# Linear attention with a leaky-ReLU layer behind it on one core: scores of stage 0 ahead of the turning of stage 1, and v*s added in whole blocks

## The chip, the cores and the metric

The kernel runs on one core of a Trainium2 chip. Its engines each work through a list of their own and wait for one another by semaphores: TensorE (PE, with its weight loads shown as PEld), VectorE (DVE), ScalarE (ACT), GpSimd (POOL) and SyncE (SP). The metric is the device time of one execution in microseconds (us). A difference is judged against runs of the kernel before on the same chip.

## The reference

```python
def _attn_ref(r, k, v, w, u):          # r, k, v: (4, 8, 768, 48); w, u: (8, 48)
    state = np.zeros((B, H, D, D))
    for t in range(S):
        cur = np.einsum('bhd,bhe->bhde', u[None] * kt, vt)
        y[:, :, t] = np.einsum('bhd,bhde->bhe', rt, state + cur)
        state = w[None, :, :, None] * state + np.einsum('bhd,bhe->bhde', kt, vt)
    return y

def _moe_ref(x, w_in, w_out):          # x: (3072, 384); w_in: (384, 2048); w_out: (2048, 384)
    h = x @ w_in
    g = np.maximum(0.01 * h, h)
    return g @ w_out
```

`x` is `y` with the heads side by side: one row of 8 x 48 = 384 for each of the 4 x 768 tokens. The term with `u` is a bonus for the token itself: token t adds v[t] times the scalar s[t] = sum over d of r*u*k, one scalar for each head.

## The kernel before

The 3072 tokens are cut into 24 stages of 128 tokens, six to a batch. The recurrence becomes chunked attention: within a stage, scores are masked to earlier tokens; across stages a state of 48 x 48 for each head is carried. A step is a letter and a stage number:

- P (`prep`, L327 and L329): VectorE scales r and k by powers of the decay into `qk`.
- T (`turn`, L379): eight matmuls against the identity turn `qk`, four for r and four for k, each half into a bank of PSUM; ScalarE (L390) copies them to `tp`; for the k half of stage 0 VectorE does it (L387).
- A (`a_mm`, L403): eight matmuls with 48 rows make the scores, two banks.
- X (`diag`, L334): VectorE multiplies the turned r and k for the scalar s.
- M (`a_mask`, L421): VectorE masks the scores into `at`. The mask is made by POOL (L267), in between its loads.
- K (`kv_mm`, L433, L437, L442): s, the products of k and v, and the carried state, in one bank.
- Q (`prep2`, L342): VectorE makes `vs`, v times s. S (`state`, L487): VectorE decays the state.
- Y (`y_part`, L522): the output of attention for a stage, turned: 384 columns of output, three blocks of 128 partitions, beside one another in one bank. ScalarE (L537) copies it into `xT`.
- G and J (L550, L567): products with w_in, ScalarE's leaky ReLU behind them. H and `second` (L584, L648): products with w_out.

In stages 0 to 7 (`n < DIAG`) the bonus comes into Y as `vs` times the identity; later stages put s on the diagonal of `at`.

Y's matmuls have 32 columns of weights each. They go to four column groups q of the array, one after the other, so that four run side by side. For each block s and group q there are one or two matmuls of `v_sb` with `at`, one of the state with `tp` (except in the first stage of a batch) and, for `n < DIAG`, one of `vs` with `ident`. That is 28 matmuls in stages 0 and 6, and 40 in stages 1 to 5 and 7.

The order of the first ten stages is written out by hand in `ORDER`. Each step adds its instructions to the lists of its engines in this order; `Sched` derives the semaphore waits from what is read and written, and an operation waits for all of its inputs before its first instruction. Banks of PSUM are taken in rotation by `next_bank`. From stage 10 on, loops over pairs of stages do the same.

Of the kernel before, what the change touches and what calls it, by code (L numbers as in the profile page):

```python
# [21 lines left out]
NSL = HD // 128  # L22
# [1 line left out]
FIRST, EARLY = 6, 2  # L24
LOADS = """r1 k1 r2 id k2 wi0 v1 r3 tri k3 v2 wi1 k4 r4 v3 wi2 k5 r5 r6 k6 v4 v5 k7 wi3 r7 v6 v7 wo3 wo2 wo1 wo0"""
ORDER = """
P0 C W T0 P1 T1 A0 X0 M0 P2 A1 K0 T2 Q0 X1 Y0 A2 S0 M1 K1 X2 G0.0 Q1 P3 S1 Y1 T3 K2 M2 G1.0 X3 A3 U G0.1 S2 G1.1 Q2 M3 Y2 K3 P4
T4 Q3 G2.0 G2.1 G0.2 S3 G2.2 G1.2 Y3 P5 A4 P6 X4 M4 T5 X5 G3.0 K4 Q4 A5 S4 T6 G3.1 K5 G3.2 Y4 M5 L8 Q5 Y5 P7 A6 G1.3 J2.0 J2.1 T7
M6 X6 X7 K6 J2.2 J2.3 A7 S6 J2.4 J2.5 L9 Q6 G2.3 G0.3 J2.6 M7 L10 J2.7 L11 G3.3 K7 S7 P8 Q7 Q8 P9 H0 Q9 K8 H1 P10 L12 K9 H2 S8 S9
Y6 Y7 A8 A9 P11 M8 H3 M9 L13  # L30
# [7 lines left out]
class Sched:  # L38
# [8 lines left out]
    def add(self, eng, emit, R=(), W=(), dma=None):  # L47
        o = Op()
        o.eng, o.emit, o.dma, o.inc, o.val = eng, emit, dma, False, None
        deps = []  # L50
        for key in R:
            w = self.writer.get(key)
            if w is not None:
                deps.append((w, True))
        for key in W:
            w = self.writer.get(key)
            if w is not None:
                deps.append((w, False))
            for r in self.readers.get(key, ()):
                deps.append((r, False))  # L60
        o.deps = []
        for d, raw in deps:
            if d.dma is None and d.eng == eng and dma is None and (eng == "pe" or not raw):
                continue
            if d is not o and d not in o.deps:
                o.deps.append(d)
        for key in R:
            self.readers.setdefault(key, []).append(o)
        for key in W:
            self.writer[key] = o  # L70
            self.readers[key] = []
        self.ops.append(o)
        return o
# [47 lines left out]
def bass_rwkv5_eagle__then__act_leaky_relu_kernel(  # L121
# [13 lines left out]
    def SB(name, shape, dt=BF16):  # L135
        return ctx.enter_context(nc.sbuf_tensor(name, shape, dt))

    NQK, NTP, NVS, NAT, NT, NX, NG, NO, NRK = 6, 6, 6, 6, 6, 3, 3, 4, 14
    TURNED, DIAG = 8, 8
# [29 lines left out]
    ident = SB("ident", [128, 128])  # L169
# [5 lines left out]
    vs = [SB(f"vs{i}", [128, HD]) for i in range(NVS)]  # L175
# [12 lines left out]
    V, A, PE, SP, G = nc.vector, nc.scalar, nc.tensor, nc.sync, nc.gpsimd  # L188
# [306 lines left out]
    def y_mm(n, ps_y, key):  # L495
        it, ia, iv, is_ = n % NTP, n % NAT, n % NVS, n % NT

        def column(q):
            todo = []
            for s in range(NSL):  # L500
                p, kk = divmod(4 * s + q, 3)
                c0 = 128 * p
                one = []
                if kk < 2:
                    one.append((v_sb[:, n, c0 + 32 * kk:c0 + 32 * kk + 32], at[ia][:, 0, p, :]))
                if kk > 0:
                    c1 = c0 + 16 + 32 * kk
                    one.append((v_sb[:, n, c1:c1 + 32], at[ia][:, 1, p, :]))
                if n % NC:
                    one.append((st[is_][:, p, 32 * kk:32 * kk + 32], tp[it][:, p, :]))  # L510
                if n < DIAG:
                    one.append((vs[iv][:, 128 * s + 32 * q:128 * s + 32 * q + 32], ident[:, :]))
                todo += [(s, a, m, i == 0, i == len(one) - 1) for i, (a, m) in enumerate(one)]
            return todo

        def emit():
            columns = [column(q) for q in range(4)]
            for step in range(max(len(x) for x in columns)):
                for q in range(4):
                    if step < len(columns[q]):  # L520
                        s, a, m, first_mm, last_mm = columns[q][step]
                        last = PE.matmul(ps_y[32 * q:32 * q + 32, 128 * s:128 * s + 128], a, m,  # L522
                                         start=first_mm, stop=last_mm)
            return last

        reads = [("v", n), "v0", ("at", ia, 0), ("at", ia, 1), "ident", ("tp", it, 0)]
        if n < DIAG:
            reads.append(("vs", iv))
        if n % NC:
            reads.append(("st", is_))  # L530
        add("pe", emit, R=reads, W=[key])

    def y_part(n):
# [328 lines left out]
```

## Time and profile before

| | |
|---|---|
| median of 3 runs | 169.61 us (168.82 to 169.82) |
| the profiled execution | 169.31 us, of which its span 167.6 us |
| PE busy | 159.8 us (95%), 2348 matmuls |
| VectorE, ScalarE, POOL busy | 120.7, 116.1, 81.7 us |
| L522 (Y), all stages | 384 with `at`, 240 with the state, 96 with `vs` |

The span is the time from the first to the last instruction of the program; the rest of the execution lies around it. "Idle before" in a group is the time in which an engine stood still ahead of it, and "<-" names what ended that. "issue" is idle time that ended with no event that the profile shows.

### The profile page before, as it was taken

How to read it: one execution, taken by the hardware profiler on the slowest of the kernel's cores; microseconds unless marked ns; L12 is line 12 of the kernel's file. 1: busy time of each engine (PE TensorE's matmuls, PEld its weight loads, DVE VectorE, ACT ScalarE, POOL GpSimd, SP SyncE). 2: the span in 40 equal slices, each digit the busy share in tenths (PEclk: the TensorE clock that was granted, in tenths of full speed). 3: DMA queues.
4: the chain of work that ended last, by engine and by line, in shares of the span. 5: the costliest groups of instructions: out<-in, count | busy, mean ns of one | idle time of the engine just before them, and what ended most of it. 6: DMA issues, size and time to landing. Idle time of an engine off the chain costs nothing.

```text
span 167.6 us, 5494 instructions
## 1 busy us (share of the span) xinstructions
PE 159.8 (95%) x2348; PEld 133.7 (80%) x2348; DVE 120.7 (72%) x232; ACT 116.1 (69%) x264; POOL 81.7 (49%) x97
## 2 busy tenths in 40 slices
PE   6679999979999999999999999999999999999994
PEld 3557898968766885886875889889899898898993
DVE  7768884853698969999449997986998477036253
ACT  4823888778323581689989889989999845828520
POOL 7999999990079979697570660840000000000000
DMA  5999999999999999989997996994507302002022
GB/s 100 112 149 172 171 152 173 202 187 143 116 123 208 109 139 75 151 150 102 203 157 42 219 124 49 215 120 77 147 0 98 125 4 94 4 0 94 4 94 94
DMA packets 99259, 19.68 MB, mean 117 GB/s; under 512 B 92322, under 2 KB 99236, under 8 KB 99236
## 3 DMA queue, kind: packets, MB, share of 16 engines
q0 software_dynamic: 76512, 10.03, 91.6%
q1 hardware_dynamic: 21682, 9.11, 26.4%
q8 instruction: 18, 0.29, 0.7%
q10 hardware_dynamic: 1042, 0.20, 0.6%
q14 instruction: 5, 0.04, 0.1%
HBM read 20.45 MB, written 4.72 MB: 150 GB/s over the span
## 4 chain that ended last, share of the span: by engine, by line
PE 93%; DVE 3%; issue 1%; ACT 1%; DVEq 0%; ACTq 0%
PE ps_all L567 31%; PE ps_all L648 20%; PE ps_all L584 16%; PE ps_all L522 7%; PE ps_all L550 7%; PE ps_all L403 4%; PE ps_all L379 3%; PE ps_all L437 3%; DVE qk L327 1%; DVE at L421 1%; PE ps_all L255 1%; PE ps_all L442 1%; PE ps_all L295 1%; PE ps_all L433 0%; DVE tp L387 0%
## 5 line engine op out<-in xcount | busy, mean ns | idle before, releaser
L567 PE MATMUL ps_all<-xT,w_in_sb 128*128 128x256 bf16 x480 | 54.5, 273 | 0.0
L567 PEld LDWEIGHTS ps_all<-xT,w_in_sb 128*128 128x128 bf16 x480 | 46.7, 98 | 5.8
L573 ACT ACTIVATE gT<-ps_all 128x512 bf16<-128x512 f32 x80 | 46.7, 595 | 5.7 <-PE ps_all L567 2.1
L218 POOL DMA_DIRECT2D rk_sb<-in_k_dram x23 | 21.7, 944 | 16.3 <-PE ps_all L567 16.3
L584 PE MATMUL ps_all<-w_out_sb,gT 128*128 128x384 bf16 x160 | 27.2, 326 | 0.0
L413 DVE CAST_PREDICATED at<-mask,ps_all 128x1024 bf16<-128x1024 uint16 x16 | 18.8, 1219 | 8.9 <-PE ps_all L403 8.9
L367 ACT ACTIVATE at<-ident,s_tok 128x128 bf16<-128x128 bf16 x80 | 24.8, 389 | 0.0
L584 PEld LDWEIGHTS ps_all<-w_out_sb,gT 128*128 128x128 bf16 x160 | 15.3, 98 | 9.7
L218 POOL DMA_DIRECT2D v_sb<-in_v_dram x24 | 22.7, 955 | 0.4 <-issue 0.4
L218 POOL DMA_DIRECT2D rk_sb<-in_r_dram x23 | 21.5, 939 | 0.0
L361 POOL TENSOR_TENSOR at<-ident,s_tok 128x512 bf16<-128x512 bf16 x12 | 13.4, 1142 | 11.6 <-DVE s_tok L351 11.6
L679 DVE TENSOR_TENSOR out_sb<-ps_all,snap 128x192 f32<-128x192 f32 x22 | 7.8, 356 | 14.5 <-PE ps_all L648 13.8
L648 PE MATMUL ps_all<-tw,gs 128*128 128x192 bf16 x168 | 16.0, 246 | 0.0
L590 ACT ACTIVATE out_sb<-ps_all 128x384 f32<-128x384 f32 x10 | 4.9, 487 | 14.6 <-PE ps_all L584 14.6
L648 PEld LDWEIGHTS ps_all<-tw,gs 128*128 128x128 bf16 x168 | 14.0, 98 | 0.0
L421 DVE TENSOR_TENSOR at<-ps_all,mask 128x512 bf16<-128x512 f32 x16 | 10.3, 684 | 4.7 <-PE ps_all L403 4.7
L537 ACT ACTIVATE xT<-ps_all 128x384 bf16<-128x384 f32 x24 | 11.0, 490 | 3.8 <-PE ps_all L522 3.4
L550 PE MATMUL ps_all<-xT,w_in_sb 128*128 128x128 bf16 x192 | 12.9, 225 | 0.0
L550 PEld LDWEIGHTS ps_all<-xT,w_in_sb 128*128 128x128 bf16 x192 | 11.8, 101 | 0.6 <-issue 0.3
L555 ACT ACTIVATE gT<-ps_all 128x512 bf16<-128x512 f32 x16 | 9.6, 599 | 3.8 <-PE ps_all L550 3.2
L522 PE MATMUL ps_all<-at,v_sb 128*32 128x128 bf16 x384 | 11.9, 224 | 0.0
L622 DVE TENSOR_TENSOR gs<-gT 128x1024 bf16<-128x1024 bf16 x14 | 9.6, 684 | 2.9 <-ACT gT L573 2.9
(81 smaller groups left out, 241.1 us busy)
## 6 DMA issues: line engine op xcount, KB each, us to landing
out_dram<-out_sb SPq DMA_DIRECT2D x22, 192.0 KB, 2.4
v_sb<-in_v_dram POOLq DMA_DIRECT2D x24, 96.0 KB, 5.8
rk_sb<-in_r_dram POOLq DMA_DIRECT2D x23, 96.0 KB, 5.7
rk_sb<-in_k_dram POOLq DMA_DIRECT2D x23, 96.0 KB, 5.3
w_in_sb<-in_moe_w_in_dram POOLq DMA_DIRECT2D x4, 384.0 KB, 6.7
w_out_sb<-in_moe_w_out_dram POOLq DMA_DIRECT2D x4, 384.0 KB, 9.9
out_dram<-out_sb SPq DMA_DIRECT2D x4, 96.0 KB, 1.6
tp<-qk SPq DMA_TRANSPOSE x16, 3.4
```

Source lines behind the costliest of these rows:

```text
L218: add("pool", lambda: G.dma_start(dst, src), R=pace, W=[key], dma=f"{which}{n}")
L361: add("pool", lambda hh=hh, s_of=s_of: G.tensor_tensor(at[ia][:, hh, :, :], ident[:, :].unsqueeze(1).to_broadcast([128, NP, 128]), s_of.un ...
L367: add("act", lambda h=h: A.activation(at[ia][:, h % 2, h // 2, :], ident[:, :], AF.Copy, scale=s_tok[n % 2][:, h:h + 1]), R=["ident", ("s" ...
L413: add("dve", lambda: V.copy_predicated(at[n % NAT][:, :, :, :].rearrange("p two m i -> p (two m) i"), mask[:, :].bitcast(mybir.dt.uint16). ...
L421: add("dve", lambda hh=hh, part=part: V.tensor_tensor(at[n % NAT][:, hh, :, :], part, mask[:, :].unsqueeze(1).to_broadcast([128, NP, 128]) ...
L522: last = PE.matmul(ps_y[32 * q:32 * q + 32, 128 * s:128 * s + 128], a, m, start=first_mm, stop=last_mm)
L537: add("act", lambda: A.activation(xT[m % NX][:, :, 128 * half:128 * half + 128], ps_y[:, 0:HD].rearrange("p (s t) -> p s t", t=128), AF.Copy),
L550: last = PE.matmul(ps_g[:, 128 * f:128 * f + 128], w_in_sb[:, s, 128 * fb:128 * fb + 128], xT[ix][:, s, t], start=s == 0, stop=s == NSL - 1)
L567: last = PE.matmul(ps_g[:, 256 * f:256 * f + 256], w_in_sb[:, s, 128 * fb:128 * fb + 128], xT[ix][:, s, :], start=s == 0, stop=s == NSL - 1)
L573: add("act", lambda: A.activation(gT[ig][:, 2 * j:2 * j + 2, :].rearrange("p f t -> p (f t)"), ps_g[:, :], AF.Prelu, alpha=0.01), R=[key], ...
L584: last = PE.matmul(ps_o[:, 0:HD], gT[ig][:, s, 128 * half:128 * half + 128], w_out_sb[:, s, :], start=s == 0, stop=s == NFB - 1)
L648: done = PE.matmul(ps_o[:, 0:NH], lhs[:, s, :], rhs[:, s, :], start=first and s == 0, stop=s == HF - 1, skip_group_check=not (first and last))
```

## The change

In `ORDER` the steps T1 and A0, and further on A1 and K0, change places. In `y_mm` the twelve matmuls of `vs` with the identity, of 32 columns each, go out of the list for the four column groups; behind it, for `n < DIAG`, three matmuls of 128 columns add them, one for each block of 128. So that these can add to what stands in the bank, the start flag is set for the first block alone in these stages, and the stop flag only on the last of the three.

```diff
 ORDER = """
-P0 C W T0 P1 T1 A0 X0 M0 P2 A1 K0 T2 Q0 X1 Y0 A2 S0 M1 K1 X2 G0.0 Q1 P3 S1 Y1 T3 K2 M2 G1.0 X3 A3 U G0.1 S2 G1.1 Q2 M3 Y2 K3 P4
+P0 C W T0 A0 P1 X0 M0 T1 P2 K0 A1 T2 Q0 X1 Y0 A2 S0 M1 K1 X2 G0.0 Q1 P3 S1 Y1 T3 K2 M2 G1.0 X3 A3 U G0.1 S2 G1.1 Q2 M3 Y2 K3 P4
 T4 Q3 G2.0 G2.1 G0.2 S3 G2.2 G1.2 Y3 P5 A4 P6 X4 M4 T5 X5 G3.0 K4 Q4 A5 S4 T6 G3.1 K5 G3.2 Y4 M5 L8 Q5 Y5 P7 A6 G1.3 J2.0 J2.1 T7
 M6 X6 X7 K6 J2.2 J2.3 A7 S6 J2.4 J2.5 L9 Q6 G2.3 G0.3 J2.6 M7 L10 J2.7 L11 G3.3 K7 S7 P8 Q7 Q8 P9 H0 Q9 K8 H1 P10 L12 K9 H2 S8 S9
 Y6 Y7 A8 A9 P11 M8 H3 M9 L13
...
                 if n % NC:
                     one.append((st[is_][:, p, 32 * kk:32 * kk + 32], tp[it][:, p, :]))
-                if n < DIAG:
-                    one.append((vs[iv][:, 128 * s + 32 * q:128 * s + 32 * q + 32], ident[:, :]))
                 todo += [(s, a, m, i == 0, i == len(one) - 1) for i, (a, m) in enumerate(one)]
...
                         s, a, m, first_mm, last_mm = columns[q][step]
                         last = PE.matmul(ps_y[32 * q:32 * q + 32, 128 * s:128 * s + 128], a, m,
-                                         start=first_mm, stop=last_mm)
+                                         start=first_mm and (s == 0 or n >= DIAG),
+                                         stop=last_mm and n >= DIAG)
+            if n < DIAG:
+                for s in range(NSL):
+                    last = PE.matmul(ps_y[:, 128 * s:128 * s + 128], vs[iv][:, 128 * s:128 * s + 128], ident[:, :],
+                                     start=False, stop=s == NSL - 1)
             return last
```

## The prediction

> **What bounds the kernel now.** I read the page first, for the engine that has no idle time to give.
>
> ```profile
> PE 159.8 (95%) x2348; PEld 133.7 (80%) x2348; DVE 120.7 (72%) x232; ACT 116.1 (69%) x264; POOL 81.7 (49%) x97
> PE   6679999979999999999999999999999999999994
> ```
>
> PE is the bound from about 12.1 us on: one slice of forty (around 35 us) is below 9 until the tail. A change that both of whose edits lie before 53 us can therefore pay in three ways only: it removes PE idle time ahead of 12 us, it removes the gap near 35 us, or it changes PE's own work. So I read next the chain of work that ended last, in order of time, for the start.
>
> ```profile
> 7.27 0.58 DVE tp L387
> 7.88 0.35 DVE qk L327
> 8.22 0.28 DVE qk L329
> 8.55 1.03 PE ps_all L379 x8
> 9.58 0.56 PE ps_all L403 x8
> 10.24 1.29 DVE at L421 x2
> 11.53 0.26 DVE qk L327
> 11.79 0.28 DVE qk L329
> 12.12 1.03 PE ps_all L379 x8
> ```
>
> L379 is a turning T, L403 the scores A, L421 the masking M, L327 and L329 the prep P. The chain runs T1, A0, M0, P2, T2: A0 has its operand from 7.96 us (the DVE cast at 7.27 takes 0.69 in the timeline) but stands on PE behind T1, which waits for P1 until 8.55. VectorE, whose list is M0, P2, Q0, X1, S0, M1, then waits 1.41 us, as its timeline shows; the third line is POOL's, which makes the mask that M0 reads:
>
> ```profile
> 8.41 0.42 DVE L334 TENSOR_TENSOR prod<-tp 128x512 bf16<-128x512 bf16 x1
> 10.24 1.29 DVE L421 TENSOR_TENSOR at<-ps_all,mask 128x512 bf16<-128x512 f32 x2 [1.41 <-PE ps_all L403]
> 8.73 0.34 POOL L267 TENSOR_SCALAR_AFFINE_SELECT mask<-ones 128x128 bf16<-128x128 bf16 x1
> ```
>
> The chain at 35 us shows the other hole, in the middle of K6's four matmuls, which wait for no semaphore:
>
> ```profile
> 35.32 0.11 PE ps_all L437 x2
> 35.43 0.93 issue
> 36.35 0.24 PE ps_all L437 x2
> ```
>
> **Edit 1, the order.** On PE, T1 A0 A1 K0 becomes A0 T1 K0 A1. The steps that issue on VectorE and ScalarE keep their order there (P1, X0, M0, P2; the copies of T1, then T2); no moved step issues a DMA, so SP and POOL are not passed, and only bank numbers change. A0 can start at 7.96 + 0.06 (the distance that T1 shows after its prep, 8.49 to 8.55) = 8.02. M0 followed A0's start by 0.72 (9.52 to 10.24), so A0 would allow 8.74; X0 ends at 8.83; the mask ends at 9.07. The mask is late next, and M0 starts at about 9.13, 1.11 earlier. T2 followed M0 by 1.88 (10.24 to 12.12), so T2 is due at 11.01. Is PE free then? A0's eight start over 0.30, and a change from A to a full-height matmul takes 0.25 in this stretch, so T1 starts at 8.57, 0.02 later than before, and its copies on ScalarE end at 10.29 in place of 10.27. K0 fits into the wait for these copies (0.33 of starts, from about 9.40); if that cover were gone it would cost these 0.33. A1 at 10.35 takes 0.30 + 0.25, and PE is free at 10.9. Behind the new head of PE's list stands only T1, whose input comes at 8.49 anyway. The loads allow it: P2's k landed at 9.94 by the trace and is read at 10.6; K1's v landed at 12.87, and K1 comes at 13.5; P3's k landed at 14.27 and is wanted at 14.8. Further on the least room is P5's r, landed 23.01 and read at 23.27 before, but M4 behind it waited 2.2 us for PE. **Edit 1: -1.11 at T2.** Bounds: 0 if the mask or T1's copies come later than I read, and -1.35 (all of VectorE's wait but its 0.06).
>
> **Edit 2, the blocks.** In stages 0 to 7 twelve matmuls of 32 columns become three of 128: 72 matmuls and 72 weight loads fewer. That is not array time saved. Four narrow ones run side by side, and the timeline of PE shows a step of four every 55 ns, while the whole blocks of L379 follow each other at 56 ns; three steps for three.
>
> ```profile
> 26.47 0.23 PE L522 MATMUL ps_all<-tp,st 128*32 128x128 bf16 x4
> 26.53 0.23 PE L522 MATMUL ps_all<-ident,vs 128*32 128x128 bf16 x4
> 26.69 0.40 PE L403 MATMUL ps_all<-tp 48*128 48x128 bf16 x8
> 27.02 0.62 PE L379 MATMUL ps_all<-ident,qk 128*128 128x128 bf16 x8
> ```
>
> What is new is a change of tile shape inside each step Y. Between two shapes the starts are 0.15 apart (26.53 to 26.69) in place of 0.056; in the slow stretch before 16.4 us it is 0.247 in place of 0.107. The trace has no narrow step followed by a whole block of the same bank; the nearest row is Y1 followed by T3, 0.152. Stages 1 and 2 go on to full blocks anyway (T3, K3), so one change only moves: 0. Stages 3, 5 and 7 go on to A (L403), another shape: +0.097 each. Stages 4 and 6 are followed directly by another Y, a joint that costs 0.127 now: 0.152 + 0.112 + 0.150 in place of 3 x 0.055 + 0.127, +0.122 each. Stage 0, slow, goes on to A2: +0.14. **Edit 2 in the array: 0.29 + 0.24 + 0.14 = +0.67.** Bounds: 0 (if a change into the same bank is free) and +4.0 (rival three). The Trainium skill (TensorEngine Tiling (Array Packing), Key Properties) says that changing the tiling mode drains the array, which speaks against this edit; the trace agrees, at 0.10 us a change, and the sum already has it.
>
> **What the smaller stream does to the gap.** 0.93 us in the chain, 1.13 between two starts where 0.04 is usual: 1.09. Nothing is waited for, and the page has a queue "instruction" with 18 packets of 0.29 MB, 16 KB each; in the trace they start at 16.1, 22.5, 28.0, 33.9 and 39.6 us. About 250 instructions of PE (matmuls, loads, waits) lie between the points 3.2 us ahead of each, and the gap ended 3.2 us ahead of the last: I read it as PE running dry of instructions. The stretch before it is the densest: Y4 and Y5 issue 160 in 1.3 us. By then 6 x 18 = 108 instructions are gone, so the same boundary comes about 4 us of PE work later, among the J steps, which need 54 ns for an instruction and not 8. The same spacing of 5.6 us between packets would nearly be reached at 31 us, for 0.3 at most. I take **-1.09**; bounds -1.09 and 0. The Trainium skill (Runtime: NRT & Kernel Launch, Instruction fetch mechanics) describes refills in blocks of 256 instructions that are mostly hidden; by "hidden" the term would be 0, but this trace shows the blocks and a visible gap.
>
> **The slow start of PE.** The granted clock is 1.00 in all rows, yet twelve matmuls of L550 take 1.42 us at 15.21 and 0.83 at 18.12 in the timeline: starts are 107 ns apart until 16.4, 56 after. If that moment stays at 16.4 while the work comes 0.97 earlier (1.11 less stage 0's 0.14), this much more work runs at half speed: +0.48. If it moves with PE's busy stretch: 0. I take the middle, +0.24.
>
> **Sum:** -1.11 + 0.67 - 1.09 + 0.24 = -1.29. The profiled execution took 169.31 (span 167.6 and 1.7 around it), so 168.0; the median of the three runs is 0.3 above it, and I forecast **168.3**. From 16 to 165 us PE carries any gain to the end: VectorE's and POOL's work from 43 us on starts from K7 on PE and shifts with it.
>
> **Rivals.**
> One: a gain does not arrive. For it: the three runs differ by 1.0 us, so the gap may not be in every run, or the instructions may be late for a reason that their number doesn't touch. Against it: the spacing of the packets. Without the gap's term: 169.61 - 0.20 = 169.4; the same without edit 1 instead.
> Two: PE reaches full speed earlier. Between 9.6 and 13.0 us PE now stands for about a third of the time; after the change it has A1, T2 and Y0 there, with holes of 0.3 us. If full speed comes at 13.0, 3.4 us of slow work shrink by 1.7, of which VectorE, with 1.6 us of idle time between 10.3 and 24.5 left over, lets perhaps 1.0 pass: 167.2. The Trainium skill (TensorE: Matmul & The Clock Gate, Part 1) gives a free-running window of 3.4 us of activity; by that rule this is a matter of phase, and the spread of the runs agrees with it.
> Three, slower: the whole blocks must wait until the narrow matmuls that wrote their columns have ended, since they add to the same words, and likewise out of them. A narrow matmul lasts 0.22, so each of 8 changes in and 7 out would cost up to 0.22 more, 3.3 in all: 168.3 + 3.3 = 171.6. It decides from 0.2 us a change. Against it: narrow groups of Y add to the same columns 0.06 us apart, with no such wait.
>
> **How the numbers follow.** The forecast 0.45 (167.7 to 168.9 by itself), rival one 0.27, two 0.20, three 0.08. A measurement of this kernel tells about 1%, 1.7 us, from no change: faster is below 167.9. Rival two nearly whole (0.17) and a third of the forecast (0.15) make 0.32; slower is most of rival three, 0.07; the rest is 0.61. The range leaves out rival three and the ends of one and two: 166.9 to 169.8.
>
> **What would show it.** M0 at 9.1 us with the mask as its releaser, T2 at 11.0; 0.15 us ahead of the whole blocks, and no saving of PE time in a step Y; no gap of "issue" on PE near 35 us; L550's first twelve at 14.3. I am wrong if M0 stays near 10.2, if a gap of about 1 us stands elsewhere on PE, or if a change of shape costs over 0.2 us.

## Result and the profile after

The changed kernel takes 168.57 us (median of 14 runs, 167.84 to 169.29) against 169.56 for the kernel before in the same job: ratio 0.9942, interval [0.9926, 0.9958], about 1.0 us faster. A second job gave 168.75 against 169.82, ratio 0.9941 [0.9913, 0.9968]. The forecast was 168.3.

The chain of the changed kernel, in order of time (start, length, what), shows the new start: A0 ahead of T1, and T2 at 10.99 where it was 12.12. L520 is now the narrow part of Y, L525 the three whole blocks.

```profile
7.27 0.70 DVE tp L387
7.97 0.05 issue
8.02 0.61 PE ps_all L403 x8
8.63 0.56 PE ps_all L379 x4
9.19 0.02 issue
9.21 1.09 ACT tp L390 x2
10.30 0.04 issue
10.35 0.61 PE ps_all L403 x8
10.96 0.04 issue
10.99 1.03 PE ps_all L379 x8
```

The masking is no longer in it. VectorE's timeline has M0 at 9.11, released by POOL's mask:

```profile
8.41 0.42 DVE L334 TENSOR_TENSOR prod<-tp 128x512 bf16<-128x512 bf16 x1
9.11 1.29 DVE L421 TENSOR_TENSOR at<-ps_all,mask 128x512 bf16<-128x512 f32 x2 [0.28 <-POOL mask L267]
```

K6 runs through without a hole (four L437 in one piece):

```profile
34.45 0.08 PE ps_all L433 x4
34.53 0.19 PE ps_all L437 x4
34.72 1.31 PE ps_all L570 x12
```

And a new wait of PE stands in its timeline near 85 us, ahead of A15, for a transpose:

```profile
84.09 0.40 PE L403 MATMUL ps_all<-tp 48*128 48x128 bf16 x8
85.50 0.40 PE L403 MATMUL ps_all<-tp 48*128 48x128 bf16 x8 [1.01 <-DMA tp<-qk]
```

Since both kernels run the same matmuls but for `vs`, each can be laid on its counterpart in the trace. The table gives how much earlier (minus) a step starts than in the profile of before, for both profiles of the changed kernel:

| step (start before) | first profile | second profile | what happened since the row above |
|---|---|---|---|
| T2 (12.12) | -1.12 | -1.13 | the new order |
| A2 (13.95) | -1.01 | -1.01 | changes of tile shape in Y0 |
| T3 (17.23) | -1.22 | -0.73 | moment at which PE reaches full speed |
| A4 (26.69) | -1.04 | -0.54 | 0.08 ahead of A3; Y3 |
| A6 (32.31) | -0.80 | -0.30 | Y4 and Y5 |
| K6, second half (36.35) | -1.88 | -1.39 | the gap in K6 is gone |
| A8 (52.54) | -1.55 | -1.06 | Y6 and Y7 |
| A15 (85.88) and on to the end | -0.37 | -1.00 | wait for the transpose |

The first profile's execution took 169.06, half a microsecond above its median; the wait ahead of A15 is what the second hardly has (0.05).

### The profile page after: what moved, and what is told of

Same layout as the page of the kernel before. It is cut to its first block, busy times and chain, and to the rows that moved or that the text cites. A ratio compares the mean times of both kernels' runs of the same rounds, so it can differ in the third digit from the quotient of the medians.

```text
span 167.2 us, 5351 instructions
## 1 busy us (share of the span) xinstructions
PE 160.3 (96%) x2276; PEld 133.6 (80%) x2276; DVE 120.6 (72%) x232; ACT 116.3 (70%) x264; POOL 81.8 (49%) x97
## 3 DMA queue, kind: packets, MB, share of 16 engines
q1 hardware_dynamic: 21682, 9.11, 26.6%
## 4 chain that ended last, share of the span: by engine, by line
PE 79%; DVE 11%; DMA 4%; issue 3%; ACT 1%; DVEq 0%; ACTq 0%
PE ps_all L570 25%; PE ps_all L651 20%; PE ps_all L587 9%; PE ps_all L553 7%; PE ps_all L520 5%; PE ps_all L403 4%; DMA tp<-qk 4%; PE ps_all L379 3%; PE ps_all L437 2%; DVE at L413 2%; DVE rku L349 2%; PE ps_all L525 1%; DVE qk L320 1%; DVE ku L347 1%; DVE tw L607 1%
## 5 line engine op out<-in xcount | busy, mean ns | idle before, releaser
L421 DVE TENSOR_TENSOR at<-ps_all,mask 128x512 bf16<-128x512 f32 x16 | 10.3, 683 | 2.2 <-PE ps_all L403 1.9
L651 PE MATMUL ps_all<-w_out_sb,gT 128*128 128x192 bf16 x112 | 11.6, 246 | 0.0
```

The costliest lines, as they stand in the source:

```text
L421: add("dve", lambda hh=hh, part=part: V.tensor_tensor(at[n % NAT][:, hh, :, :], part, mask[:, :].unsqueeze(1).to_broadcast([128, NP, 128]) ...
L651: done = PE.matmul(ps_o[:, 0:NH], lhs[:, s, :], rhs[:, s, :], start=first and s == 0, stop=s == HF - 1, skip_group_check=not (first and last))
```

## Experiments

Times stand beside runs of the kernel before in the same job: 169.91 (first four runs) and 169.82 (last four).

### The order alone

The start of `ORDER`'s first line; the rest of it stays:

```diff
-P0 C W T0 P1 T1 A0 X0 M0 P2 A1 K0 T2
+P0 C W T0 A0 P1 X0 M0 T1 P2 K0 A1 T2
```

> The new order alone; Y as before. Theory (the gap at K6 comes from the number of PE's instructions): M0 at 9.1 us, T2 at 11.0, but the gap of about 1.1 us in K6 stays, since all 2348 matmuls are there: about 168.5 us, 1.1 below before. Rival (the gap goes with the earlier time of K6, not with the instructions): no gap, 167.4 us.

168.88 us, ratio 0.9949 [0.9928, 0.9970]: 0.9 faster by the ratio. T2 comes 1.13 earlier, and the gap in K6 is still there, in the chain in order of time:

```profile
34.26 0.11 PE ps_all L437 x2
34.36 1.15 issue
35.51 0.26 PE ps_all L437 x2
```

It has grown, from 1.13 us between two starts to 1.35. K6 running earlier does not remove it: the growth takes 0.22 of what the order gives. In this profile PE also loses 0.27 ahead of A13, to a transpose that landed late. The rival falls.

### The blocks alone

```diff
-                if n < DIAG:
-                    one.append((vs[iv][:, 128 * s + 32 * q:128 * s + 32 * q + 32], ident[:, :]))
...
+            if n < DIAG:
+                for s in range(NSL):
+                    last = PE.matmul(ps_y[:, 128 * s:128 * s + 128], vs[iv][:, 128 * s:128 * s + 128], ident[:, :],
+                                     start=False, stop=s == NSL - 1)
```

> The whole blocks alone; order as before. Theory: M0 at 10.2 us as before, the gap in K6 gone (-1.1), the changes of tile shape cost 0.8 as in the trace of the changed kernel: about 169.2 us, 0.3 below before. Rival (the gap goes with the time): it stays, 170.3 us, 0.8 above before.

169.41 us, ratio 0.9972 [0.9951, 0.9993]: 0.5 faster, where the theory had 0.3 and the rival a loss. The chain passes K6 without a hole, though here it comes at about the time of before:

```profile
35.72 0.19 PE ps_all L437 x4
```

Against before, steps here lie 0.40 later at A6, 0.69 earlier behind K6 and 0.36 earlier at A8: the blocks' own work is a loss, and the gap pays for it. At A15 they lie 0.24 later again: PE waits 0.60 there for the same transpose as in the changed kernel.

### As many instructions as before, in whole blocks

```diff
                 for s in range(NSL):
-                    last = PE.matmul(ps_y[:, 128 * s:128 * s + 128], vs[iv][:, 128 * s:128 * s + 128], ident[:, :],
-                                     start=False, stop=s == NSL - 1)
+                    for c in range(0, 128, 32):
+                        last = PE.matmul(ps_y[:, 128 * s + c:128 * s + c + 32], vs[iv][:, 128 * s:128 * s + 128],
+                                         ident[:, c:c + 32], start=False, stop=s == NSL - 1 and c == 96)
```

> The changed kernel with each whole block cut into four matmuls of 32 moving columns: twelve for a stage again, so as many PE instructions as before the change, same order and same changes of tile shape. The pieces cost array time: 12 x 0.027 in place of 3 x 0.056, 0.16 for a stage, 1.2 in all. Theory (number of instructions): the gap of about 1.1 us near 34 us comes back besides: 170.9 us. Rival: no gap, 169.8 us.

169.59 us, ratio 0.9992 [0.9977, 1.0008]. By its time alone this would be the rival's run (169.8). The trace says otherwise; the gap is back in the same place, but smaller:

```profile
35.46 0.11 PE ps_all L437 x2
35.57 0.45 issue
36.02 0.26 PE ps_all L437 x2
```

My 170.9 was too high in part because I had brought the gap back at its full 1.1 us. The slower pieces (A6 is 0.14 later than before, where the changed kernel is 0.80 earlier) give the instructions time to arrive: 0.65 between two starts is left. The pieces themselves cost 0.13 for a stage (stages 2 to 7), not 0.16, and PE does not wait ahead of A15 here, where the changed kernel loses 0.05 or 1.18.

In the three kernels with as many matmuls ahead of K6 as before, the gap comes at the same place in PE's list, behind 1217 or 1218 recorded PE instructions; in the seven other profiles, with 50 or 54 matmuls fewer ahead of K6, there is none. The packets on the "instruction" queue go with its end. In all three, PE goes on 2.4 us after the start of a packet of 16 KB: 33.95 and 36.35 us before, 33.13 and 35.51 with the order alone, 33.64 and 36.02 here. In the other seven the same matmul starts 0.4 to 1.0 us after the start of the packet, without a hole. That settles what the gap hangs on: the instruction's number, and how fast PE got there.

### Whole blocks ahead of the narrow matmuls

```diff
+            whole = n < DIAG
+            ahead = whole and n not in (5, 7)
...
+            if ahead:
+                blocks()
             for step in range(max(len(x) for x in columns)):
...
+            if whole and not ahead:
+                last = blocks()
```

> The changed kernel with the three whole blocks ahead of the narrow matmuls in stages 0 to 4 and 6, where the step before Y is made of whole blocks already (stages 5 and 7, which follow another Y, keep them behind). Theory (a change of tile shape costs about 0.1 us, 0.14 in the slow stretch, and nothing else): the extra changes of stages 0, 3, 4 and 6 go away, about 0.45 us: 168.1 us. Rival (what costs is adding whole blocks and narrow matmuls to the same columns): no gain, 168.6 us.

167.94 us, ratio 0.9887 [0.9863, 0.9912], against 0.9942 for the changed kernel in the first job: about 0.9 us better than it by the ratios, where 0.45 was due. Between T2 and A2 nothing is lost now (-1.12 at both), at A4 neither; Y4 with Y5 and Y6 with Y7 cost 0.11 each in place of 0.24 and 0.33. With the 0.08 ahead of A3, that is 0.11 + 0.08 + 0.10 + 0.13 + 0.22 = 0.64. The rest I can only suppose to be A15, where PE waits 0.06 in this profile. In the chain, the whole blocks of stages 4 and 5 now stand at the outer ends of the pair, at 30.54 and 31.69 us, with the 56 narrow matmuls between them.

### The changed kernel again, and the same instruction boundaries further on

> The changed kernel once more, for a second profile and for times beside the next ones. Theory (a refill of PE's instructions falls among the transposes of stages 14 and 15 in every kernel with 2276 matmuls): the last of these two transposes lands 5.7 us or more after its issue again, and PE waits about 1 us ahead of A15 near 84 us. Rival (a chance delay of that profile): it lands in 3.4 us and PE does not wait. Time 168.6 us either way.

The last transpose of the pair landed 5.7 us after its issue, in the first profile 6.8. The other half of that expectation was wrong: PE waited 0.05 us and not 1. That PE was 0.5 later here did not help it, since the pair was issued 0.5 later too: in both profiles the last issue comes 5.8 us before A15 could start. A15 starts 0.13 us after the landing, so only what a transpose takes beyond 5.67 us is lost, and this one took 1.1 us less. The same sum gives, to 0.02, the waits at A15 in the profiles of the blocks alone (0.60), the blocks first (0.06) and the early mask (0.61), though the profile puts the first and the last of these down to ScalarE. 168.75 us.

The next run has 72 matmuls of two columns behind H0.

```diff
-P9 H0 Q9
+P9 H0 Z72 Q9
...
+            for _ in range(n):
+                last = PE.matmul(ps[i][:, 0:2], ones[:, 0:128], ones[:, 0:2], start=True, stop=True)
```

> The changed kernel with 72 matmuls of two columns behind H0, which compute nothing that is used: as many PE instructions from there on as before the change, for 1.9 us of PE time (72 x 0.026). Theory (the refill among the transposes): the refill goes back out of the stretch of the transposes of stages 14 and 15, the last of them lands 3.4 us after its issue, and PE has no wait ahead of A15. Rival (the transposes are late for another reason): it lands after 5.7 us or more as in the changed kernel.

The transpose landed 3.5 us after its issue, and PE does not wait. A single run, the profiled one, took 170.37 us. The two transposes are on SP's queue; its timeline for the changed kernel, first profile, and for this run (the second column is from the first issue to the end of the second on the queue):

```profile
77.25 4.39 SPq L322 DMA_TRANSPOSE tp<-qk  x2
```

```profile
79.81 2.69 SPq L332 DMA_TRANSPOSE tp<-qk  x2
```

Over all profiles, the delay of the second transpose and the packets of 16 KB on the "instruction" queue nearest to it:

| kernel | matmuls | issue to landing | packets of instructions at |
|---|---|---|---|
| before; order alone; pieces; this one | 2348 | 3.4; 3.3; 3.5; 3.5 | 75.2, 87.4; 75.3, 86.3; 76.2, 87.6; 76.1, 88.9 |
| after; again; blocks alone; blocks first; early mask | 2276 | 6.8; 5.7; 6.2; 5.7; 6.3 | 78.6; 80.1; 79.7; 79.6; 78.6 |
| with fills | 2280 | 4.0 | 78.2 |

Where a packet falls between the issue of the pair (77 to 80 us) and its landing, the transpose takes two to three microseconds more; the kernel with fills, whose packet starts just ahead of the second issue, shows little of it. The loads are not the difference: in the changed kernel's first profile and in this run the last of POOL's loads is issued 1.1 us ahead of the pair and the next 2.7 us behind it.

Stage 18's transpose gives a check in the other direction. In the four kernels with 2348 matmuls a packet starts 1.1 to 1.7 us behind its issue, and it lands after 4.7 to 5.4 us; in the other six profiles none starts before it lands, and it takes about 3.4. But a transpose can be slow without a packet: stage 13's takes 5.0 to 7.1 us in all ten profiles, with none in it. Why one packet delays a transpose that long no run shows.

### An earlier mask, and a PE that does not rest

Both edits are made to the blocks-first kernel; the first is a part of `LOADS`:

```diff
-wi0 v1 r3 tri k3 v2
+wi0 tri v1 r3 k3 v2
```

> Whole blocks first as in the run before, and the mask made one load ahead on POOL, before the loads of v of stage 1 and r of stage 3. Theory (the mask is what M0 waits for in the changed kernel): M0 at 8.9 us in place of 9.1; T2 gains 0.1 at most, since A1 stands on PE until 10.9: 167.8 us, about 0.8 below the changed kernel in the same job. Rival: the loads behind the mask come later and cost what it gives, 168.0.

168.04 us, ratio 0.9903 [0.9867, 0.9940], beside 0.9941 for the changed kernel in the same job. M0 comes at 8.66, but T2 only 0.18 earlier than in the changed kernel, part of it from a start that was 0.07 earlier. Against the blocks-first kernel (0.9887) no gain is measured. Its profile shows where a gain would go: full speed came early in it, at 14.1 us, and at A8 PE is 1.16 ahead of the blocks-first profile. Then it waits for two transposes, 0.89 us ahead of A9 and 0.61 ahead of A15. PE's timeline has the first wait:

```profile
51.10 0.40 PE L403 MATMUL ps_all<-tp 48*128 48x128 bf16 x8 [0.72 <-DMA tp<-qk]
```

The second edit, on top of the early mask, at the start of `ORDER`'s first line:

```diff
-P0 C W T0 A0 P1 X0 M0 T1 P2 K0 A1
+P0 C W F1 T0 F2 A0 P1 X0 M0 T1 P2 K0 F1 A1
```

> The kernel with the early mask, and four matmuls of 512 columns in the idle stretches of PE before 10.4 us: one ahead of T0, two between T0 and A0, one ahead of A1. Theory (full speed comes a stretch of some 3.4 us after PE is busy throughout): the moment at which starts go from 107 to 56 ns moves from 15 to 16.4 us to 10 to 13 us, worth 0.5 to 1.0: about 167.1 us. Rival (the moment does not depend on these holes): no change against the early mask, or 0.1 lost.

167.56 us, ratio 0.9878 [0.9844, 0.9912], 0.5 below the early mask; the two intervals overlap. What the run tells clearly is in its trace. PE's timeline has T1 and T2 (L379, eight matmuls each) with the last of the four fills and A1 between them:

```profile
8.48 1.03 PE L379 MATMUL ps_all<-ident,qk 128*128 128x128 bf16 x8
9.74 0.63 PE L255 MATMUL ps_all<-ones 128*128 128x512 bf16 x1
10.30 0.42 PE L403 MATMUL ps_all<-tp 48*128 48x128 bf16 x8
10.65 0.62 PE L379 MATMUL ps_all<-ident,qk 128*128 128x128 bf16 x8
```

T2 takes 0.62 where it took 1.03 in both kernels. Full speed comes by 10.3 us; in the other nine profiles the last slow matmul starts between 14.1 and 16.8. So it does hang on how busy PE was, and 2.8 us are won by the end of the first G step. Yet at A3 only 1.6 are left: PE then waits for a load that the faster start has caught up with (in the list of waits):

```profile
PE ps_all L433 <- DMA v_sb<-in_v_dram: 0.9, 1, 0.9
PE ps_all L403 <- DMA tp<-qk: 0.5, 1, 0.5
```

The second line is A9's wait again, which costs 0.71 in all. At A8 this profile (-2.51) and that of the early mask (-2.56), where full speed came at 14.1, are level, so by then nothing is left of what the fills won.

## Why the prediction was right, and where it was off

**Edit 1 in the order: right, -1.12 for -1.11.** M0 was released by the mask at 9.11, foretold 9.13; T2 at 10.99, foretold 11.01. The second part of PE's wait was read right as well: making the mask earlier brings little, since T1's copies hold A1 until 10.35.

**Edit 2 in the array: a loss, but under-sized.** Foretold +0.67, seen in the first profile 0.11 + 0.08 + 0.10 + 0.24 + 0.33 = 0.86. The price of one change of shape was right; PE's timeline has 0.16 from the last narrow step to the whole blocks in Y3:

```profile
25.22 0.23 PE L520 MATMUL ps_all<-tp,st 128*32 128x128 bf16 x4
25.38 0.34 PE L525 MATMUL ps_all<-ident,vs 128*128 128x128 bf16 x3
25.65 0.40 PE L403 MATMUL ps_all<-tp 48*128 48x128 bf16 x8
```

Missed were the 0.08 that PE now loses ahead of A3 and 0.11 of Y6 and Y7. A3 waits for ScalarE's copies of T3, which stand behind its copy of Y1; that copy now waits 0.18 us for the whole blocks at Y1's end. Of the 0.11, 0.07 is a misread joint: between Y4 and Y5 the narrow matmuls start 0.13 apart (31.51 and 31.64 us before), and the sum took this for Y6 and Y7 too, but there PE's timeline of before has the usual step:

```profile
51.82 0.23 PE L522 MATMUL ps_all<-ident,vs 128*32 128x128 bf16 x4
51.88 0.23 PE L522 MATMUL ps_all<-at,v_sb 128*32 128x128 bf16 x4
```

Rival three, whole blocks that wait for the narrow ones to end, is refuted by the rows of Y3.

**The gap in K6: right in size (-1.09) and in cause.** It stayed with the order alone, went with the blocks alone, and came back at the same instruction with the blocks in pieces, ending each time 2.4 us after the start of a packet of instructions. The Trainium skill (Runtime: NRT & Kernel Launch, Instruction fetch mechanics) says that instructions come in blocks of 256 and that this is mostly hidden; the trace agrees with the blocks (252 to 255 recorded instructions of PE from packet to packet, as the mean of each profile), and 0.65 to 1.35 us were not hidden where Y's matmuls are dense.

**The slow start: the middle was a fair choice.** The last slow matmul starts at 14.8 and 15.9 us in the two profiles of the changed kernel, and at 16.3 in that of before. Against an unmoved shift of -1.01 this made -0.21 and +0.28, foretold +0.24; that is the half microsecond between the two profiles. The run with 72 small matmuls, whose start is the same, has +0.55. So the bounds, 0 and +0.48, were too narrow on both sides, and their middle lies near the mean of the three. The Trainium skill (TensorE: Matmul & The Clock Gate, Part 1) has a free-running window of 3.4 us; kernels with the same start differ here by 1.8 us (14.8 to 16.7), which agrees. Rival two came true only with the fills, and then VectorE was not what stopped it, as I had said, but a load of v.

**What the sum did not have: the transposes.** "From 16 to 165 us PE carries any gain to the end" failed at A15, for 1.18 us in the first profile and 0.05 in the second. I had followed what the smaller stream does to the gap, and not where its other boundaries would fall. So forecast -1.29, measured about -1.0. In the second profile the sum misses about 0.3: 0.19 in the array, 0.05 at A15 and 0.04 in the slow start. In the first it misses 0.92: 0.19 and 1.18, less the 0.45 by which full speed came earlier. How long that transpose takes was outside the forecast, so that the median lies near the second profile is in that part luck.

The two parts alone gave 0.9 and 0.5 us; together they gave 1.0, which their intervals don't separate from the sum of 1.4.

## What to carry to other kernels

On an engine with a long unrolled stream, count instructions as well as time: a hole in the middle of an operation that waits for nothing may be the stream itself running late, and a denser step ahead of it is the place to shorten. Matmuls that change the tile shape cost about 0.1 us at each change, so put those of one shape beside neighbours of the same shape; by the trace that was worth 0.64 us here, while the blocks alone brought 0.5. And a gain on the bounding engine has to be followed to the next transfer that it will catch up with.

## What the runs showed of the hardware

One packet of 16 KB for PE's instructions among the transposes went with a landing at 5.7 to 6.8 us in place of 3.3 to 3.5, in five profiles against four; at stage 18 it was 4.7 to 5.4 in place of 3.4, in four profiles against six. When PE ran out of instructions, it went on 2.4 us after the start of a packet, in all three profiles with a gap. And four matmuls of 512 columns in PE's idle time brought its full speed from 14.1 to 16.8 us forward to about 10, while the granted clock in the profile reads 1.00 throughout.
